# Sliding-window attention into a leaky-ReLU MLP: two zero fills moved from GpSimd to VectorE, one value cast shared between ScalarE and GpSimd, and one attention step placed a quarter tile later

## The chip, the core and the metric

The kernel runs on one core of a Trainium2 chip. The core has five engines that run their own instruction streams in order and wait for each other by semaphores: TensorE (PE; its weight loads are listed as PEld), VectorE (DVE), ScalarE (ACT), GpSimd (POOL) and SyncE (SP), which here only starts DMAs. The metric is device time in microseconds (us); the time before is the median of three runs.

## What is computed

Attention over a band of 32 positions on either side, for 8 batches, 8 heads, 576 positions and 64 values per head; then two dense layers with a leaky ReLU between, over all 4608 tokens:

```python
scores = scale * np.matmul(q, k.transpose(0, 1, 3, 2))
mask = np.abs(pos[:, None] - pos[None, :]) <= window      # window = 32
scores = np.where(mask, scores, -1000000000.0)
...
attn = attn / (np.sum(attn, axis=-1, keepdims=True) + 1e-09)
attn_out = np.matmul(attn, v)
x = attn_out.transpose(0, 2, 1, 3).reshape(B * S, H * D)   # 4608 x 512
h = x @ w_in                                              # 512 x 2048
g = np.maximum(0.01 * h, h)
out = g @ w_out                                           # 2048 x 512
```

## The kernel before

**Tiling.** Heads are taken in pairs (p = 0 to 3), and a batch's 576 positions in two halves of 288 tokens. An attention *step* i handles one pair in one half of one batch: batch i // 8, half (i // 4) % 2, pair i % 4; there are 64 steps. Keys and values of a pair lie block-diagonally: `kbd[b % 2]` and `vbd[b % 2]` are [128 partitions, pair, 9 blocks, 128], where head 0 fills the upper left 64 x 64 of each block, head 1 the lower right, and the rest must be zero. There are two copies of each, for even and odd batches. The copies for batch 0 are zeroed at the start (lines 134 to 137 and 158), those for batch 1 by POOL memsets of [128, 1152] in bf16: the four of `kbd[1]` and pairs 0 and 1 of `vbd[1]` at line 543, pairs 2 and 3 of `vbd[1]` at line 567. Later batches write only the diagonal parts again.

**A step** (`step`, line 420) issues: `join(i+1)` on DVE, which adds the two halves of the next step's masked scores (only from i = 11 on); `score(i+2)`, five matmuls into the single PSUM tile `ps`, the exponential on ACT (line 280) and the mask product on POOL (line 282); `sums(i)` on PE and the reciprocal on DVE (line 309); `product(i)`, five matmuls of `vbd` with the masked exponentials (line 320) into the single PSUM tile `x`; `scaled(i)` on DVE (line 334), which writes the attention output `xT`. Then keys that have arrived are copied into `kbd` on DVE (`place_keys`, line 258 for batches 0 and 1, line 260 later), and casts, transposes and loads of later batches are issued as `qk_due` and `v_due` tell (for batch 2 from step 9 on).

**Inputs.** Float32 loads are started by SP: `qf` and `kf` per pair, `vf` per pair in two transfers, one for each head. `cast_qk` casts queries on the engine given, else POOL, and keys on POOL (line 197); `cast_v` casts values into `vbd`, one instruction for each head, on ACT (line 203) or POOL (line 205). For batches 0 and 1 the cast tiles are transposed on PE (line 225) and copied out of PSUM by ACT (lines 233 and 239); from batch 2 on, DMAs transpose.

**The dense layers.** A group g is half a batch: 288 tokens, and 16 `h` tiles (line 348, four matmuls each) whose leaky ReLU ACT writes to `gT` (line 355). An `o` tile is 128 tokens by 512 outputs, 16 matmuls (line 390), copied out by ACT (line 395) and stored by SP. The `h` tiles, the `o` tiles, the transposes of PE and nothing else share four PSUM buffers (`mmps`). PE's order is that of the program text.

**The order around the change.** After group 0's tiles with steps 4 to 7 between them, DVE casts the queries of batch 1's pairs 0 and 1 (lines 558 and 559), and group 1's tiles follow (lines 560 to 569), with `second_pair(0)` and `second_pair(1)` behind tiles 7 and 11: transposes of a pair on PE, its copies on ACT, its keys' placing on DVE, then `cast_qk` of the pair two further on, queries on DVE and keys on POOL. The memsets of line 567 are issued behind tiles 7 and 9, and `score(8)` behind tile 13. From there a planned order runs: `plan` lists quarters of `o` tiles (four matmuls each) and `h` tiles; ahead of each `spend` is called. It counts the calls in `turn` and keeps a clock in estimated time; whenever the first entry of `due` has come, it issues the next step. `O_US` is the estimate for a quarter `o` tile. Step 8's entry is `4 * O_US`, which is the fifth turn, the first quarter of output tile 1; steps 9, 10 and 11 are at turns 8, 11 and 13. Ahead of steps 8 to 10 the values of pairs 1 to 3 of batch 1 are cast on ACT. The turns 1, 2 and 4 add `second_pair(2)`, `score(9)`, and `second_pair(3)` with the value cast of pair 0.

Of the kernel before, what the change touches and what calls it, by code (L numbers as in the profile page):

```python
# [16 lines left out]
def kernel(  # L17
# [14 lines left out]
    nc = tc.nc  # L32
# [54 lines left out]
    def load_v(b, p):  # L87

        t = fload.tile([128, NB, D], FP32, name=f"vf{p}")
        for a in range(2):  # L90
            nc.sync.dma_start(
                out=t[64 * a:64 * a + 64],
                in_=v[b, 2 * p + a].rearrange("(c p) d -> p c d", p=64),
            )
        vf[b, p] = t
# [25 lines left out]
    vbd = [const.tile([128, NPAIR, NB, 128], BF16, name=f"vbd{i}") for i in range(2)]  # L121
# [64 lines left out]
    def cast_qk(b, p, q_eng=None):  # L186
        for eng, src, dst in ((q_eng or nc.gpsimd, qf, qb), (nc.gpsimd, kf, kb)):
            if b < BY_DMA:
                parts = [(dst[:, p], src[b, p].rearrange("p a (c d) -> p c a d", d=D))]
            else:  # L190
                by_c = src[b, p].rearrange("p a (g c d) -> c p g a d", g=3, c=2)
                parts = [(dst[:, p, 3 * c:3 * c + 3], by_c[c]) for c in range(2)]
            for to, tok in parts:
                if eng is nc.scalar:
                    eng.activation(out=to, in_=tok, func=AF.Copy)
                else:
                    eng.tensor_copy(out=to, in_=tok)  # L197

    def cast_v(b, p, on_act=False, heads=range(2)):
        for a in heads:  # L200
            r = slice(64 * a, 64 * a + 64)
            if on_act:
                nc.scalar.activation(out=vbd[b % 2][r, p, :, r], in_=vf[b, p][r], func=AF.Copy)  # L203
            else:
                nc.gpsimd.tensor_copy(out=vbd[b % 2][r, p, :, r], in_=vf[b, p][r])  # L205
# [64 lines left out]
    def score(i):  # L270
        b, hf, p = where(i)
        by_c = qT[b][:, p].rearrange("p (c i) -> p c i", c=2)
        for n_, blocks in enumerate(WIN[hf]):
            for blk, i0, n in blocks:
                nc.tensor.matmul(  # L275
                    ps_v[:, n_, :, i0:i0 + n], kbd[b % 2][:, p, blk],
                    by_c[:, :, hf * EVEN + i0:hf * EVEN + i0 + n], start=True, stop=True,
                )
        e = attn.tile([128, 2 * HALF], BF16, name="e")
        nc.scalar.activation(out=e, in_=ps[:, P0:P0 + 2 * HALF], func=AF.Exp, scale=scale)  # L280
        pr = prob[:, i % NPROB]
        nc.gpsimd.tensor_mul(  # L282
            pr.rearrange("p n c i -> p (n c i)"), e, mask[hf].rearrange("p n c i -> p (n c i)"),
        )
        probs[i] = [pr, None, None]
# [60 lines left out]
    def h_mms(g, f, h, cs):  # L346
        for c in cs:
            nc.tensor.matmul(  # L348
                h[:, 0:HALF], w_in_bf[:, c, ts(f, 128)], xT[:, c, ds(g * HALF % RING, HALF)],
                start=(c == 0), stop=(c == DMC - 1),  # L350
            )

    def h_out(g, f, h):

        nc.scalar.activation(  # L355
            out=gT[:, f, ds(g * HALF % RING, HALF)].rearrange("p (i c) -> p i c", c=2),
            in_=h[:, 0:HALF].rearrange("p (c i) -> p i c", c=2), func=AF.Prelu, alpha=0.01,
        )

    def h_tile(g, f, n=1):  # L360

        hs = [mmps.tile([128, 512], FP32, name="mm", tag="mm") for _ in range(n)]
        for cs in (range(DMC - 1), (DMC - 1,)) if n > 1 else (range(DMC),):
            for i, h in enumerate(hs):
                h_mms(g, f + i, h, cs)
        for i, h in enumerate(hs):
            h_out(g, f + i, h)

    def h_first(g):

        hs = [mmps.tile([128, 512], FP32, name="mm", tag="mm") for _ in range(4)]
        yield hs[0]
        for c in range(DMC):
            for f in range(4):
                h_mms(g, f, hs[f], (c,))
            if c == DMC - 1:
                for f in range(4):
                    h_out(g, f, hs[f])
            yield
# [40 lines left out]
    def step():  # L420


        i = state["done"]
        if JOINED - 1 <= i < NC - 1:
            join(i + 1)
        if i < NC - 2:
            score(i + 2)
        weighted(i)
        place_keys()
        for b, p in qk_due.get(i, ()):  # L430
            cast_qk(b, p)
            transpose_dma(b, p)
            if 2 < b < B - 1:
                load_qk(b + 1, p)
        if 12 < i <= 12 + NPAIR:
            load_qk(3, i - 13)
        for b, p in v_due.get(i, ()):
            cast_v(b, p)
            if b + 1 < B:
                load_v(b + 1, p)  # L440
        state["done"] += 1
# [104 lines left out]
    def second_pair(p):  # L546
        next(second)
        next(second)
        place_keys()
        if p + 2 < NPAIR:  # L550
            cast_qk(1, p + 2, nc.vector)
            load_qk(2, p)
        if p == 1:
            load_qk(2, 2)
            load_qk(2, 3)

    second_half()
    cast_qk(1, 0, nc.vector)
    cast_qk(1, 1, nc.vector)
    for _ in h_first(1):  # L560
        pass
    for f in range(4, FFC):
        h_tile(1, f)
        if f in (7, 11):
            second_pair((f - 7) // 4)
        if f in (7, 9):
            nc.gpsimd.memset(vbd[1][:, (f - 3) // 2], 0.0)
        if f == 13:
            score(8)

# [3 lines left out]
    H_US, O_US, LEAD = 4 * (HALF / 2400 + 2.5e-3), 4 * 0.216, 4.0  # L574
# [9 lines left out]
    for us, kind, g, f in plan:  # L584
        if kind == "h" and f == 0:
            at[g] = t
        t += us
    due = [O_US * n for n in (4, 7, 10, 12)]
    for i in range(12, NC):
        prev = at[i // 4 - 1] - LEAD + (1.8 if i < 16 else 0)  # L590
        due.append(prev + (at[i // 4] - LEAD - prev) * (i % 4 + 1) / 4)
# [3 lines left out]
    def spend(us):  # L595
        nonlocal clock, turn
        while due and due[0] <= clock + 1e-6:
            due.pop(0)
            i = state["done"]
            if i < 11:  # L600
                cast_v(1, i - 7, on_act=True)
            step()
            if 10 <= i < 14:
                load_v(2, i - 10)
        turn += 1
        if turn == 1:
            second_pair(2)
        if turn == 2:
            score(9)
        if turn == 4:  # L610
            second_pair(3)
            cast_v(1, 0, on_act=True)
        clock += us

    for us, kind, g, f in plan:
        if kind == "h":
            spend(us)
            if f != 0:
                h_tile(g, f - 1, 2) if f == 1 else h_tile(g, f)
        elif f == 0:  # L620
            o_tile(g, lambda: spend(O_US))
# [28 lines left out]
```

## Time and profile before

| what | before |
|---|---|
| time, median of 3 runs | 320.3 us (319.94 to 320.85) |
| profiled execution, first to last instruction | 319.0 us |
| PE busy | 301.1 us (94%), granted clock 1.000 |
| DVE, ACT, POOL busy | 220.7, 183.5, 191.2 us |
| 0 to 36 us: PE busy | 24.30 us |
| 36 to 66 us: PE busy | 27.83 us |
| 300 to 319 us: PE busy | 15.82 us |

The profiled execution is not one of the three timed runs; its span is what its own instructions cover, and no separate time is recorded for it. All times within a run are counted from the span's start. A row of the order of time gives the start, the time from that start to the end of the last of its instructions, the engine, the source line, the operation, the tiles it writes and reads, and how many instructions are merged; in brackets stands how long the engine stood idle before and what ended that. Ends of matmuls are modelled, so neighbouring matmuls overlap in such rows, and a few matmul records are missing from the trace.

### The profile page before, as it was taken

Reading aid. Unit: us, or ns where it says so; the run is one execution under the profiler, and the core shown is the slowest. Engines: PE = TensorE matmul, PEld = TensorE weight load, DVE = VectorE, ACT = ScalarE, POOL = GpSimd, SP = SyncE. Lnnn points to the kernel's source line nnn. Section 1 sums busy time; section 2 is a strip of 40 time slices with the busy share of each in tenths; the row PEclk is TensorE's granted clock in tenths of the full one; section 3 lists DMA queues with packets and bytes.
Section 4 is the critical chain, followed back from the end, with each engine's and each line's share of the span. In section 5 each row is a group of like instructions: output and inputs, shape, how many; then the busy total and the mean of one; then the engine's idle time right before and its main releaser. Section 6 shows DMA issues by size and latency. Waiting matters only on the chain.

```text
span 319.0 us, 6455 instructions
## 1 busy us (share of the span) xinstructions
PE 301.1 (94%) x2429; PEld 203.5 (64%) x2449; DVE 220.7 (69%) x258; ACT 183.5 (58%) x394; POOL 191.2 (60%) x251
## 2 busy tenths in 40 slices
PE   2678998999999999999999999999999999999996
PEld 1457764576765858576765858576665858576653
DVE  5688886869755987688755987688745988565100
ACT  7686688574652828375552828465552837464531
POOL 7899963974646866585646866586637866330000
PEclk9999999999999999999999999999999999999999
DMA  8999998997998989399835996399833440000102
GB/s 189 224 184 229 269 242 188 242 200 180 223 245 167 245 148 210 79 237 202 173 76 114 233 229 151 74 215 223 178 76 104 108 71 33 35 35 2 66 31 71
DMA packets 108400, 49.46 MB, mean 155 GB/s; under 512 B 68816, under 2 KB 103888, under 8 KB 108368
## 3 DMA queue, kind: packets, MB, share of 16 engines
q1 hardware_dynamic: 104144, 44.84, 66.0%
q0 software_dynamic: 4224, 4.19, 8.1%
q8 instruction: 19, 0.31, 0.5%
q14 instruction: 13, 0.11, 0.1%
HBM read 36.70 MB, written 9.44 MB: 145 GB/s over the span
## 4 chain that ended last, share of the span: by engine, by line
PE 88%; DVE 5%; ACT 3%; issue 2%; POOL 1%; ACTq 0%; POOLq 0%; DVEq 0%
PE mm L390 38%; PE mm L348 37%; PE x L320 5%; PE ps L275 5%; PE s L301 2%; DVE r L309 2%; DVE qb L197 1%; PE s L304 1%; DVE kbd L258 1%; POOL prob L282 1%; ACT kT L239 1%; PE tp L225 1%; ACT e L280 1%; ACT vbd L203 1%; DVE kbd L134 1%
## 5 line engine op out<-in xcount | busy, mean ns | idle before, releaser
L309 DVE RECIPROCAL r<-s 128x288 f32<-128x288 f32 x64 | 125.2, 1956 | 57.0 <-PE s L301 53.3
L282 POOL TENSOR_TENSOR prob<-e,mask 128x576 bf16<-128x576 bf16 x64 | 81.6, 1276 | 89.2 <-ACT e L280 42.1
L348 PE MATMUL mm<-xT,w_in_bf 128*128 128x288 bf16 x1024 | 134.0, 286 | 0.1
L390 PE MATMUL mm<-w_out_bf,gT 128*128 128x512 bf16 (+2 forms) x572 | 128.7, 373 | 1.1
L355 ACT ACTIVATE gT<-mm 128x288 bf16<-128x288 f32 x256 | 101.2, 412 | 25.6 <-PE mm L348 9.1
L348 PEld LDWEIGHTS <-w_in_bf 128*128 128x128 bf16 x1024 | 98.4, 98 | 24.5 <-issue 0.3
L390 PEld LDWEIGHTS <-gT 128*128 128x128 bf16 x592 | 56.3, 98 | 59.2
L395 ACT ACTIVATE o_sb<-mm 128x512 f32<-128x512 f32 (+2 forms) x37 | 21.7, 585 | 91.8 <-PE mm L390 89.0
L280 ACT ACTIVATE e<-ps 128x576 bf16<-128x576 f32 x64 | 41.5, 648 | 10.6 <-PE ps L275 10.5
L197 POOL CAST kb<-kf 96x384 bf16<-96x384 f32 (+1 forms) x56 | 34.8, 643 | 4.5 <-DMA kf<-in_k_dram 4.3
L205 POOL CAST vbd<-vf 64x576 bf16<-64x576 f32 x50 | 34.7, 694 | 1.5
L334 DVE TENSOR_TENSOR xT<-x,r 128x288 bf16<-128x288 f32 x64 | 29.2, 457 | 7.8 <-PE x L320 1.1
L260 DVE COPY kbd<-kT 64x576 bf16<-64x576 bf16 x48 | 32.3, 674 | 0.6 <-DMA kT<-kb 0.3
L320 PE MATMUL x<-prob,vbd 128*128 128x128 bf16 (+2 forms) x320 | 26.0, 213 | 2.7 <-ACT vbd L203 1.3
L275 PEld LDWEIGHTS <-kbd 128*128 128x128 bf16 x320 | 20.8, 99 | 10.7 <-DVE kbd L258 1.6
L275 PE MATMUL ps<-qT,kbd 128*128 128x128 bf16 (+2 forms) x320 | 26.3, 214 | 1.3 <-DVE kbd L258 0.8
L197 POOL CAST qb<-qf 96x384 bf16<-96x384 f32 x48 | 24.4, 536 | 0.0
L320 PEld LDWEIGHTS <-vbd 128*128 128x128 bf16 x320 | 20.5, 99 | 5.4 <-ACT vbd L203 1.9
L292 DVE TENSOR_TENSOR both<-prob 128x288 bf16<-128x288 bf16 x52 | 20.0, 384 | 0.9
L301 PE MATMUL s<-both,ones_bd 128*128 128x288 bf16 x52 | 14.9, 286 | 0.0
L258 DVE COPY kbd<-kT 64x576 bf16<-64x576 bf16 x16 | 7.1, 446 | 6.2 <-ACT kT L239 6.0
L225 PE MATMUL tp<-ident,qb 96*128 96x96 bf16 x48 | 4.1, 233 | 6.8 <-DVE qb L197 6.8
(43 smaller groups left out, 87.9 us busy)
## 6 DMA issues: line engine op xcount, KB each, us to landing
qf<-in_q_dram SPq DMA_DIRECT2D x32, 288.0 KB, 4.6
kf<-in_k_dram SPq DMA_DIRECT2D x32, 288.0 KB, 5.3
vf<-in_v_dram SPq DMA_DIRECT2D x64, 144.0 KB, 4.4
out_dram<-o_sb SPq DMA_DIRECT2D x35, 256.0 KB, 3.9
w_in_bf<-in_moe_w_in_dram POOLq DMA_DIRECT2D x4, 512.0 KB, 8.2
w_out_bf<-in_moe_w_out_dram POOLq DMA_DIRECT2D x4, 512.0 KB, 16.4
qT<-qb SPq DMA_TRANSPOSE x24, 4.2
kT<-kb SPq DMA_TRANSPOSE x24, 3.1
```

Source lines behind the costliest of these rows:

```text
L197: eng.tensor_copy(out=to, in_=tok)
L205: nc.gpsimd.tensor_copy(out=vbd[b % 2][r, p, :, r], in_=vf[b, p][r])
L260: nc.vector.tensor_copy(out=to.rearrange("p n (m c) -> p n c m", c=2), in_=kT[r].rearrange("p (c n m) -> p n c m", c=2, n=NB),)
L275: nc.tensor.matmul(ps_v[:, n_, :, i0:i0 + n], kbd[b % 2][:, p, blk], by_c[:, :, hf * EVEN + i0:hf * EVEN + i0 + n], start=True, stop=True,)
L280: nc.scalar.activation(out=e, in_=ps[:, P0:P0 + 2 * HALF], func=AF.Exp, scale=scale)
L282: nc.gpsimd.tensor_mul(pr.rearrange("p n c i -> p (n c i)"), e, mask[hf].rearrange("p n c i -> p (n c i)"),)
L309: nc.vector.reciprocal(r, s)
L320: nc.tensor.matmul(x_v[:, :, i0:i0 + n], vbd[b % 2][:, p, blk, :], pr[:, n_, :, i0:i0 + n], start=(blk == parts[0][1]), stop=(blk == parts ...
L334: nc.vector.tensor_mul(place(i), x, r)
L348: nc.tensor.matmul(h[:, 0:HALF], w_in_bf[:, c, ts(f, 128)], xT[:, c, ds(g * HALF % RING, HALF)], start=(c == 0), stop=(c == DMC - 1),)
L355: nc.scalar.activation(out=gT[:, f, ds(g * HALF % RING, HALF)].rearrange("p (i c) -> p i c", c=2), in_=h[:, 0:HALF].rearrange("p (c i) -> ...
L390: nc.tensor.matmul(o[:, lo:hi], gT[:, f, ds(128 * j % RING, 128)], w_out_bf[:, f, lo:hi], start=(f == 0), stop=(f == FFC - 1),)
```

## The change

Three places change. The two memsets of pairs 2 and 3 of `vbd[1]` leave POOL's stream, where they stood among group 1's tiles, and are issued on DVE right behind its casts of the queries of pairs 0 and 1. The first entry of `due` becomes `5 * O_US`, so that step 8, with the value cast of pair 1 that goes ahead of it, is issued one turn later. And of the value cast of pair 0 in batch 1, head 0 stays on ACT while head 1 goes to POOL.

```diff
     cast_qk(1, 0, nc.vector)
     cast_qk(1, 1, nc.vector)
+    for p in (2, 3):
+        nc.vector.memset(vbd[1][:, p], 0.0)
     for _ in h_first(1):
         pass
     for f in range(4, FFC):
         h_tile(1, f)
         if f in (7, 11):
             second_pair((f - 7) // 4)
-        if f in (7, 9):
-            nc.gpsimd.memset(vbd[1][:, (f - 3) // 2], 0.0)
         if f == 13:
             score(8)
...
-    due = [O_US * n for n in (4, 7, 10, 12)]
+    due = [O_US * n for n in (5, 7, 10, 12)]
...
             second_pair(3)
-            cast_v(1, 0, on_act=True)
+            cast_v(1, 0, on_act=True, heads=(0,))
+            cast_v(1, 0, heads=(1,))
```

## The prediction

> **What bounds the kernel now.** I read the page's busy shares first (PE 94%, every other engine at 69% or less), then PE's busy time stage by stage, then who PE waited for, then each engine's order of time around those waits. By stage:
>
> ```profile
> 66.00:100.00 34.00, 33.84 (x273) 22.80 (x274) 25.04 (x30) 19.29 (x44) 18.57 (x24) 1.00 1.08 198
> 100.00:200.00 100.00, 99.68 (x803) 68.06 (x808) 77.36 (x93) 56.38 (x128) 68.19 (x91) 1.00 0.82 175
> ```
>
> The columns are stretch, length, then busy us of PE, its weight loads, DVE, ACT and POOL, granted clock, DMA share and GB/s. From 66 us on PE is busy without a hole, at clock 1.00, and no wait of PE is listed after 60 us. So work that PE starts earlier at 66 us ends earlier by as much. The change touches 35 to 52 us, and between 40 and 60 us PE waited twice:
>
> ```profile
> PE x L320 <- ACT vbd L203: 1.1, 1, 1.1
> PE tp L225 <- DVE qb L197: 0.7, 1, 0.7
> ```
>
> These are the first values product of batch 1 (step 8) waiting for its values, and the transposes of pair 2 waiting for DVE's cast of their queries. Those two waits are all that can be won. In order of time on PE:
>
> ```profile
> 45.07 0.43 PE L225 MATMUL tp<-ident,qb 96*128 96x96 bf16 x6 [0.66 <-DVE qb L197]
> 51.54 0.41 PE L320 MATMUL x<-prob,vbd 128*128 128x96 bf16 x5 [1.09 <-ACT vbd L203]
> ```
>
> **The fills.** DVE, and below it POOL, in that stretch:
>
> ```profile
> 37.74 1.17 DVE L197 CAST qb<-qf 96x768 bf16<-96x768 f32 x1
> 40.86 0.91 DVE L258 COPY kbd<-kT 64x576 bf16<-64x576 bf16 x2 [1.96 <-ACT kT L239]
> 41.80 3.21 DVE L197 CAST qb<-qf 96x768 bf16<-96x768 f32 x1
> 44.94 0.89 DVE L258 COPY kbd<-kT 64x576 bf16<-64x576 bf16 x2
> 45.86 2.11 DVE L197 CAST qb<-qf 96x768 bf16<-96x768 f32 x1
> ```
>
> ```profile
> 38.44 1.15 POOL L197 CAST kb<-kf 96x768 bf16<-96x768 f32 x1
> 41.79 0.82 POOL L197 CAST kb<-kf 96x768 bf16<-96x768 f32 x1 [2.19 <-DMA kf<-in_k_dram]
> 42.55 2.05 POOL L567 MEMSET vbd<- 128x1152 bf16 x2
> 45.50 0.82 POOL L197 CAST kb<-kf 96x768 bf16<-96x768 f32 x1 [0.90 <-DMA kf<-in_k_dram]
> ```
>
> The same DVE cast takes 0.64 us at its shortest (at 6.83 us) and 3.21 at 41.80. It ends at 45.01, 0.41 behind the end of POOL's fills (42.55 + 2.05 = 44.60). The cast at 37.74 ends at 38.91, 0.42 behind POOL's cast that ended at 38.49; the one at 45.86 ends at 47.97, 0.42 behind POOL's mask product that ended at 47.55. So DVE's cast stands still while POOL works, and comes out 0.42 us after it. With the fills gone from POOL, only the key cast (to 42.61) stands beside the cast at 41.80: it ends near 43.03 instead of 45.01. PE's work before the transposes ends at 44.41 (eight matmuls from 43.27, 1.14 us), so they start there and not at 45.07: **0.66 won**. What is late next: their PSUM buffers, which ACT empties with the last two of its copies until 45.00; the first of the two by about 44.6, when the second group of six transposes asks for it (44.41 + 0.26). I put that at 0, with 0.1 as its bound.
>
> On DVE the fills cost little. Its memsets of zero run as 32-bit words: 128x64 took 0.112 us, and the big one is
>
> ```profile
> 2.76 1.98 DVE L134 MEMSET kbd<- 128x2304 uint32 x1 [0.43 <-issue]
> ```
>
> which makes (1.978 - 0.112)/(2304 - 64) = 0.83 ns a word, so 576 words take 0.54 us, two 1.08: from 38.91 to 39.99. Were they as slow as POOL's (1.05 each), 41.01. What hides them is DVE's idle 1.96 us before 40.86, where it waits for ACT's first keys; at the slow bound the key copy comes 0.15 later, and the cast behind it has 1.38 to spare before 44.41. So 0 at both ends. Behind the fills on DVE stand only that copy and that cast. Nothing has read or written this part of vbd[1] before, so no wait is added. On POOL nothing else moves: the key cast at 45.50 and the mask products behind it hang on a DMA that lands at 45.47 (issued 28.67, 16.8 to landing).
>
> **The step, and the cast in halves.** ACT's order of time before:
>
> ```profile
> 49.43 0.65 ACT L239 ACTIVATE kT<-tp 128x576 bf16<-128x576 bf16 x1
> 50.09 1.39 ACT L203 ACTIVATE vbd<-vf 64x576 bf16<-64x576 f32 x2
> 51.51 0.60 ACT L395 ACTIVATE o_sb<-mm 128x512 f32<-128x512 f32 x1
> 52.13 1.39 ACT L203 ACTIVATE vbd<-vf 64x576 bf16<-64x576 f32 x2
> 53.54 0.65 ACT L280 ACTIVATE e<-ps 128x576 bf16<-128x576 f32 x1
> ```
>
> Step 8 before: score(10) on PE at 49.80, sums(8) at 50.04; product(8) could follow at 50.28 and came at 51.54, behind both casts: **1.26 lost**, more than the 1.09 listed because matmul ends are modelled. Moving the step from turn 5 to turn 6 puts four output matmuls (0.87 us, the step from 48.93 to 49.80) ahead of it. The step issues no DMA, and neither ACT's, DVE's, POOL's nor SP's order changes: it is moved past these four matmuls alone. New times, all 0.66 earlier to begin with: third pair's keys on ACT end at 49.42; the one half cast there ends near 50.12; the other half stands on POOL behind mask product 9 (47.68 + 1.42 = 49.10) and ends at 49.76 (0.66, the median of POOL's value casts; at their longest, 0.91, 50.01). Both halves of the source have landed by 48.7 (issued 31.27 and 33.52, 17.0 and 15.2 to landing). Step 8 now starts at 49.80 - 0.66 + 0.87 = 50.01, its product at 50.49: no wait. So the gross gain is 0.66 + 1.26 = **1.92**.
>
> **The new wait.** Between steps 8 and 9 there are now 8 matmuls (1.73) and not 12 (2.59), so score(11) comes at 50.73 + 1.73 = 52.46. It overwrites the scores that exp(10) reads, and exp(10) stands on ACT behind the half cast, one output copy and both casts for pair 1: 50.12 + 0.62 + 1.41 + 0.65 = 52.80. PE waits till about 52.85: **0.39 given back**. (Before, exp(10) ended at 54.19 and score(11) came at 54.38.) Product(9) also overwrites what scaled(8) reads. Reciprocal(8) starts with sums(8), at 50.70, ends at 52.66; scaled(8) ends at 53.23 if it follows as others do (0.10 after), in time for product(9) at 53.33. But before it came late:
>
> ```profile
> 53.58 0.46 DVE L334 TENSOR_TENSOR xT<-x,r 128x288 bf16<-128x288 f32 x1 [0.51 <-DVE r L309]
> ```
>
> 0.51 after its reciprocal, with nothing named as cause. If that comes again, product(9) waits 0.35 more. Steps 10 and 11 show 0.10, so I take none, and 0.35 as the bound. Behind step 9 there are 12 matmuls again; step 11 keeps the 0.32 it loses now (its product at 60.95, behind scaled(10), which ends at 60.90).
>
> **Sum:** -0.66 - 1.26 + 0.39 = -1.53 us; with the late scaling -1.18. Against the profiled span, 319.0 becomes 317.5. The runs shown have a median of 320.3 (319.94 to 320.85), 1.3 above that span; taking the same off it gives **318.8**.
>
> **Rivals.**
> *No new wait (0.14).* ACT reaches exp(10) in time, as when its copies come some tenths sooner: the whole 1.92 stays, 318.4. For it: the margin is 0.39 in a chain of five instructions. Against: ACT has no idle in it to give.
> *POOL's half is locked out (0.10).* DVE's key copies for pair 3 stand at about 49.5 to 50.4. If they get in ahead of POOL's cast as POOL gets in ahead of DVE's casts, the half ends at 50.4 + 0.66 = 51.1, product(8) waits 0.6, and exp(10) is then no longer last: 1.92 - 0.6 = 1.3 won, 319.0. For it: POOL's key cast takes 0.82 alone, 1.15 beside DVE's; against: the 16 copies of this kind never ran over 0.45, and POOL should start its cast 0.4 earlier than they. The Trainium skill, "SBUF — State Buffer", section "Who interferes with whom", says that DVE copies in a two-port mode and GpSimd instructions take a shared port pair for a whole instruction, and that whoever issues second is blocked fully; the 0.42 us above agree with it for DVE's casts, and no row here shows it for POOL's value cast behind a key copy.
> *The cast is not freed (0.12).* If the 3.21 is not the fills' doing, the transposes stay at 45.07, everything behind them is 0.66 later with its margins unchanged, and the gain is 1.26 - 0.39 = 0.87: 319.4. Against it stand the three 0.42s. Smaller versions, in which a later wait hides the rest, lie between that and 320.3 (0.06).
> *Slower (0.08): the transfers don't come earlier.* POOL's first query and key casts of batch 2 stand ahead of mask product 12, join(12) on DVE waits for that, and behind the join stand reciprocal(11) and scaled(11), which the last chunk of the next h tiles needs. The keys of that cast land at 56.7 (issued 51.48, 5.2 to landing); POOL would ask for them at 57.1 instead of 58.5. Scaled(11) would end at 62.3 and is needed at 63.85 (64.64 - 1.53 + 0.74), so a landing decides from 0.4 + 1.55 = 1.95 us later, and the kernel is slower from 1.95 + 1.53 = 3.5. With the 9.1 us that a load issued at 26.2 took, it lands 3.9 later: 320.7. For it: POOL waited 2.19 and 0.90 for such loads just before. Against: the loads' issue is not delayed by anything in the change.
>
> **How the numbers follow.** My forecast has 0.50. About 0.3% (0.96 us, down to 319.34) is what this measurement can tell from no change. The forecast and the first two rivals are faster: 0.74, less 0.02 for the edge of the third; the cast not freed and its smaller versions are the same: 0.18, plus 0.02; slower 0.08. Range 318.0 (all 1.92 and 0.36 for the spread of the runs before) to 320.2, which leaves out the slower case and the edges. The forecast's own range is 318.4 to 319.2.
>
> **What would show it.** Right: DVE's cast at 41.8 lasts about 1.2; the fills lie in 38.9 to 40.0; the transposes of pair 2 start near 44.4 unwaited; product(8) follows sums(8) by 0.24; score(11) waits for exp(10) some 0.4. Wrong: a cast still over 2 us, product(8) waiting for POOL, a wait on DVE's scaling at step 9, or any PE wait after 60 us that is not there now.

## The result and the profile after

The changed kernel takes 319.13 us (median of 5 runs, 318.88 to 319.14) against 320.3 (319.85 to 320.85): a ratio of 0.9963, 95% interval 0.995 to 0.9976, or 1.2 us less (0.8 to 1.6). The forecast was 318.8 in 318.0 to 320.2. The profiled span falls from 319.0 to 317.4.

The page's head and PE's busy time by stretch after (columns as before):

```profile
span 317.4 us, 6460 instructions
...
PE 301.6 (95%) x2429; PEld 204.0 (64%) x2449; DVE 218.3 (69%) x260; ACT 182.3 (57%) x393; POOL 189.3 (60%) x250
```

```profile
36.00:66.00 30.00, 29.56 (x255) 19.33 (x256) 20.83 (x26) 22.09 (x46) 19.35 (x26) 1.00 1.16 234
66.00:100.00 34.00, 33.84 (x262) 22.12 (x263) 25.62 (x32) 17.88 (x40) 19.91 (x26) 1.00 1.10 202
100.00:200.00 100.00, 99.68 (x813) 68.47 (x819) 76.74 (x92) 57.62 (x131) 66.42 (x90) 1.00 0.82 174
```

From 36 to 66 us PE is busy 29.56 us instead of 27.83; from 66 to 200 us its busy time is what it was (33.84 and 99.68). DVE in order of time, with the fills:

```profile
39.18 1.15 DVE L561 MEMSET vbd<- 128x576 uint32 x2
41.08 0.91 DVE L258 COPY kbd<-kT 64x576 bf16<-64x576 bf16 x2 [0.76 <-ACT kT L239]
...
42.02 1.18 DVE L197 CAST qb<-qf 96x768 bf16<-96x768 f32 x1
43.55 0.91 DVE L258 COPY kbd<-kT 64x576 bf16<-64x576 bf16 x2 [0.36 <-ACT kT L239]
44.49 0.56 DVE L197 CAST qb<-qf 96x768 bf16<-96x768 f32 x1
```

The two fills (line 561) take 1.15 us and end at 40.33, 0.75 before the key copy that waits for ACT. The cast of pair 2's queries, which took 3.21 us, takes 1.18, and that of pair 3's, which took 2.11, takes 0.56. PE around steps 8 and 9:

```profile
44.47 0.42 PE L225 MATMUL tp<-ident,qb 96*128 96x96 bf16 x6
...
50.05 0.40 PE L275 MATMUL ps<-qT,kbd 128*128 128x96 bf16 x5
50.29 0.41 PE L304 MATMUL s<-prob,ones_bd 128*128 128x288 bf16 x2
50.54 0.40 PE L320 MATMUL x<-prob,vbd 128*128 128x96 bf16 x5
50.77 1.89 PE L390 MATMUL mm<-w_out_bf,gT 128*128 128x512 bf16 x7
52.65 0.40 PE L275 MATMUL ps<-qT,kbd 128*128 128x96 bf16 x5
52.89 0.41 PE L304 MATMUL s<-prob,ones_bd 128*128 128x288 bf16 x2
53.31 0.40 PE L320 MATMUL x<-prob,vbd 128*128 128x96 bf16 x5
```

Neither wait of before is left. Product(8) follows sums(8) by 0.25. What is new is small: score(11) comes 1.88 behind the start of the eight matmuls that take 1.73, so it waits 0.15; product(9) comes 0.42 behind sums(9) and not 0.24, so it waits 0.18. ACT and DVE show for what:

```profile
49.49 0.68 ACT L203 ACTIVATE vbd<-vf 64x576 bf16<-64x576 f32 x1
50.08 0.57 ACT L395 ACTIVATE o_sb<-mm 128x512 f32<-128x512 f32 x1
50.55 1.37 ACT L203 ACTIVATE vbd<-vf 64x576 bf16<-64x576 f32 x2
51.95 0.65 ACT L280 ACTIVATE e<-ps 128x576 bf16<-128x576 f32 x1
```

```profile
50.74 1.96 DVE L309 RECIPROCAL r<-s 128x288 f32<-128x288 f32 x1 [0.27 <-PE s L304]
52.80 0.46 DVE L334 TENSOR_TENSOR xT<-x,r 128x288 bf16<-128x288 f32 x1
```

Exp(10) ends at 52.60 and score(11) starts at 52.65; scaled(8) ends at 53.26 and product(9) starts at 53.31.

One measure serves all runs below: the *stretch*, the time from the first transposes of batch 1 (line 225) to the first matmul of group 2's `h` tiles (line 348), both on PE. All that the change moves lies in it. It was 64.64 - 39.06 = 25.58 us and is 63.08 - 39.28 = 23.80: 1.78 less. Behind it the two profiled executions agree within 0.04 us (254.36 and 254.32); ahead of it the new one is 0.22 longer, which makes the span's 1.6. Each kernel has one traced execution, and that of before is one of its longer ones; what this does to the comparison stands under *The sum* below.

### The profile page after: what moved, and what is told of

It reads as the page before. It is cut to its first block, busy times and chain, and to the rows that moved or that the text cites. A ratio compares the mean times of both kernels' runs of the same rounds, so it can differ in the third digit from the quotient of the medians.

```text
span 317.4 us, 6460 instructions
## 1 busy us (share of the span) xinstructions
PE 301.6 (95%) x2429; PEld 204.0 (64%) x2449; DVE 218.3 (69%) x260; ACT 182.3 (57%) x393; POOL 189.3 (60%) x250
## 4 chain that ended last, share of the span: by engine, by line
PE 91%; DVE 4%; ACT 2%; issue 1%; POOL 1%; POOLq 0%; ACTq 0%; DVEq 0%
PE mm L348 39%; PE mm L390 38%; PE ps L275 5%; PE x L320 5%; PE s L301 2%; DVE r L309 2%; PE s L304 1%; PE tp L225 1%; ACT e L280 1%; POOL prob L282 1%; DVE kbd L134 1%; DVE kbd L258 1%; ACT kT L239 0%; ACT vbd L203 0%; DVE qb L197 0%
```

## The experiments

The ratio of each is to runs of the kernel before on the same chip. A stretch is read from the one traced execution, which need not be a typical one: for "all but the fills" it took 320.34 us (median 319.57), for the steps and batch 2's casts later 318.56 (median 320.6).

| kernel | stretch, us | median, us | ratio, 95% interval |
|---|---|---|---|
| before | 25.58 | 320.08 to 320.3 | 1 |
| changed | 23.80 | 319.13 | 0.9963 (0.995 to 0.9976) |
| changed, once more | 23.80 | 319.18 | 0.9966 (0.9953 to 0.9978) |
| fills only | 24.75 | 320.07 | 0.9991 (0.9979 to 1.0002) |
| all but the fills | 25.00 | 319.57 | 0.9985 (0.9975 to 0.9994) |
| cast whole on ACT | 24.60 | 319.92 | 0.9987 (0.9978 to 0.9997) |
| step 8 not later | 24.12 | 319.45 | 0.9977 (0.9967 to 0.9986) |
| fills in POOL's idle time | 24.21 | 319.52 | 0.9973 (0.9962 to 0.9984) |
| the same, two small DVE memsets | 23.80 | 319.13 | 0.9971 (0.9956 to 0.9986) |
| next value cast halved too | 23.80 | 319.14 | 0.9972 (0.9958 to 0.9986) |
| steps 9 to 11 later too | 23.16 | 319.04 | 0.9958 (0.9946 to 0.997) |
| ... and batch 2's casts later | 23.16 | 320.6 | 0.9997 (0.9967 to 1.0026) |
| batch 2's casts later alone | 24.55 | 319.84 | 0.9985 (0.9964 to 1.0005) |
| steps later, one pair's casts later | 23.16 | 320.78 | 1.002 (1.001 to 1.003) |

### The parts one by one

**Fills only.** Against the changed kernel:

```diff
-    due = [O_US * n for n in (5, 7, 10, 12)]
+    due = [O_US * n for n in (4, 7, 10, 12)]
...
-            cast_v(1, 0, on_act=True, heads=(0,))
-            cast_v(1, 0, heads=(1,))
+            cast_v(1, 0, on_act=True)
```

> Only the fills move to DVE; step 8 stays at turn 5 and both value casts of pair 0 stay on ACT. Measured by the stretch on PE from the first transposes of batch 1 to the first matmul of group 2: 25.58 us before (39.06 to 64.64), 23.80 in the changed kernel (39.28 to 63.08). Theory (the two waits are separate terms): the transposes of pair 2 start unwaited, 0.66 is won, product(8) still waits for ACT's two casts by 1.26: stretch 24.92, median near 319.6. Rival (once the keys come earlier the values come early enough too): stretch 23.8 to 24.0, median near 319.1. Rival (the 3.21 us cast is not the fills' doing): stretch 25.58, median 320.3.

Stretch 24.75, 0.83 won: the theory's 0.66 and 0.17 more. Product(8) still waits, 1.09 by the list. The transposes of pair 2 start at 44.47 as in the changed kernel, where that is 0.98 behind the start of the eight matmuls ahead of them (43.49), while the listed end of those is 1.14 behind; the idle time of 0.66 that was listed before was really 0.82. By the ratio the runs are only 0.29 us below before (0.06 above to 0.67 below), and by the medians 0.04 (320.07 and 320.11): in the median run moving the fills alone won nothing. More on that under *The sum*.

**All but the fills.**

```diff
-    for p in (2, 3):
-        nc.vector.memset(vbd[1][:, p], 0.0)
...
+        if f in (7, 9):
+            nc.gpsimd.memset(vbd[1][:, (f - 3) // 2], 0.0)
```

> The cast in halves and the later step, with the fills left on POOL where they were. Theory: the DVE cast of pair 2's queries again lasts about 3.2 us and the transposes behind it wait 0.66; product(8) waits for nothing, and step 9 keeps its two short waits (0.15 for exp(10), 0.18 for scaled(8)): stretch 23.80 + 0.66 = 24.46, median near 319.8. Rival (POOL's half of the cast is late, as the fills keep POOL busy): product(8) waits for POOL, stretch over 25.

Stretch 25.00 instead of 24.46. The cast lasts 3.19 again and the transposes wait for it. The rest comes from something that the expectation had left out, the pause before scaled(8) that the kernel before had shown; first DVE, then PE:

```profile
42.02 3.19 DVE L197 CAST qb<-qf 96x768 bf16<-96x768 f32 x1
...
54.01 0.46 DVE L334 TENSOR_TENSOR xT<-x,r 128x288 bf16<-128x288 f32 x1 [0.51 <-PE ps L275]
```

```profile
53.70 0.41 PE L304 MATMUL s<-prob,ones_bd 128*128 128x288 bf16 x2
54.52 0.40 PE L320 MATMUL x<-prob,vbd 128*128 128x96 bf16 x5 [0.41 <-DVE xT L334]
```

Product(9) waits for that scaling: 0.82 behind sums(9) instead of the changed kernel's 0.42, which is 0.40; its transposes of pair 2 start 0.79 later than the changed kernel's (45.27 - 39.29 against 44.47 - 39.28), the rest of the 1.20. POOL's half of the cast was in time (49.37 to 50.03), so the rival fell.

**The cast whole on ACT, and step 8 not later.** One edit each:

```diff
-            cast_v(1, 0, on_act=True, heads=(0,))
-            cast_v(1, 0, heads=(1,))
+            cast_v(1, 0, on_act=True)
```

> As the changed kernel, but both value casts of pair 0 on ACT. Theory: the second cast ends 0.68 later, near 50.85 in the changed kernel's time, so product(8) waits about 0.36; everything behind it on ACT is 0.68 later too, exp(10) ends near 53.28 and score(11) comes at 53.33, product(9) at 53.81 instead of 53.31: stretch 24.30, median near 319.6. Rival (the quarter tile alone covers the casts): stretch 23.80.

```diff
-    due = [O_US * n for n in (5, 7, 10, 12)]
+    due = [O_US * n for n in (4, 7, 10, 12)]
```

> As the changed kernel, but step 8 stays at turn 5. Theory: product(8) could come at 49.68 (in the changed kernel's time) and waits for ACT's half cast, which ends near 50.17: 0.5 lost; but with 12 matmuls to step 9 again neither exp(10) nor scaled(8) is late there, so 0.33 comes back: stretch 23.80 + 0.2 = 24.0, median near 319.3. Rival (the later step is worth its full quarter, 0.87): stretch 24.6.

With the cast whole, the stretch is 24.60, 0.3 above the theory: product(8) waits as expected (0.39 by its starts), but exp(10) ends at 53.63 and not at 53.28: from the start of pair 0's cast to the next cast behind it ACT needs 2.03 (49.54 to 51.57) and in the changed kernel 1.06 (49.49 to 50.55), 0.97 more and not 0.68. So half a cast is worth 0.80 us. With step 8 at its old turn the stretch is 24.12: product(8) waits 0.47 by the list, the waits at step 9 are gone, and 0.32 remains. The later quarter tile is worth 0.3, not its 0.87.

The run with step 8 not later also shows who holds up whom when DVE's cast comes first. DVE, then POOL:

```profile
42.02 0.56 DVE L197 CAST qb<-qf 96x768 bf16<-96x768 f32 x1
```

```profile
42.09 1.17 POOL L197 CAST kb<-kf 96x768 bf16<-96x768 f32 x1 [2.27 <-DMA kf<-in_k_dram]
```

Here the keys landed 0.07 us after DVE's cast had begun: DVE takes 0.56 and POOL's cast 1.17. In the changed kernel POOL's began at 41.96, 0.06 ahead of DVE's: POOL 0.82, DVE 1.18. The first to start runs at full speed, the other one waits for it. The Trainium skill says this in "SBUF — State Buffer", section "Who interferes with whom": the shared port pair goes to whoever issues first, for a whole instruction. The trace agrees, with these four numbers.

Which of the two is first is not fixed for a kernel. In the trace of the changed kernel once more (the last run below) DVE's cast began at 42.02 and took 0.56, and POOL's came second:

```profile
42.09 1.17 POOL L197 CAST kb<-kf 96x768 bf16<-96x768 f32 x1 [2.28 <-DMA kf<-in_k_dram]
```

### Why POOL, and what the pause is

**Fills in POOL's idle time.**

```diff
     for p in (2, 3):
-        nc.vector.memset(vbd[1][:, p], 0.0)
+        nc.gpsimd.memset(vbd[1][:, p], 0.0)
```

> As the changed kernel, but the two fills stay on POOL and are issued right behind its key casts of pairs 0 and 1, where POOL stands idle for 2.2 us until the next keys land. Theory A (what counts is that the fills no longer stand beside DVE's cast of pair 2): that cast lasts 0.6 to 1.2 us and the transposes behind it start unwaited, as in the changed kernel. Theory B (the pause of 0.5 us before DVE's scaling of step 8 comes with the place in DVE's instruction stream, which is again that of the kernel before): scaled(8) starts 0.5 after its reciprocal, product(9) waits 0.4 longer than in the changed kernel: stretch 24.2, median near 319.5. Rival to B (the pause came from the fills on POOL or from the late transposes): no pause, stretch 23.80, median near 319.1. Rival to A (the fills must leave POOL): stretch 24.6 or more.

**The same with two small instructions on DVE.**

```diff
     for p in (2, 3):
         nc.gpsimd.memset(vbd[1][:, p], 0.0)
+        nc.vector.memset(zero, 0.0)
```

> As the run before it (fills on POOL in its idle time), with two more instructions on DVE at the place where the changed kernel has its fills: memsets of one column that is zero already. They do nothing but move the instructions behind them two places on in DVE's stream. Theory B: the pause before scaled(8) is gone as in the changed kernel, stretch 23.80, median near 319.1. Rival: the stretch is that of the run before it, 24.2 if a pause was there.

The first gives 24.21, the second 23.80, as theories A and B had it. DVE's cast of pair 2 took 0.56 in both. Scaled(8) without and with the two small memsets:

```profile
53.09 0.46 DVE L334 TENSOR_TENSOR xT<-x,r 128x288 bf16<-128x288 f32 x1 [0.51 <-PE ps L275]
```

```profile
52.58 0.46 DVE L334 TENSOR_TENSOR xT<-x,r 128x288 bf16<-128x288 f32 x1
```

Without them it starts 0.51 behind its reciprocal (50.62 + 1.96 = 52.58), with them 0.10 (50.52 + 1.96 = 52.48). Their work is nothing; they move what follows two places on in DVE's stream. The other traces fit: scaled(8) starts 0.51 behind its reciprocal in the kernel before and in "all but the fills", which have no such two instructions, and 0.10 or 0.11 behind in all that have them. So the fills need not leave POOL, they need only not stand beside DVE's cast; and of the changed kernel's 1.78, 0.41 is the pause that two more instructions on DVE push elsewhere. In the changed kernel pauses of 0.48 and 0.47 stand before the scalings at 166.92 and 282.24, where PE waits for nothing. The Trainium skill, "Runtime: NRT & Kernel Launch", section "Instruction fetch mechanics", says that engines fetch instructions in blocks and that crossing a block's end is mostly hidden; a pause bound to a place in the stream fits that, but no run here counts instructions to a block's end.

### Step 9's new wait, and a better order

**The next value cast halved too.**

```diff
-                cast_v(1, i - 7, on_act=True)
+                cast_v(1, i - 7, on_act=True, heads=(0,) if i == 8 else range(2))
+                if i == 8:
+                    cast_v(1, 1, heads=(1,))
```

> As the changed kernel, but the next value cast too (pair 1, issued with step 8) is halved between ACT and POOL. Theory (two things are late at step 9, exp(10) and, behind it, scaled(8)): exp(10) ends 0.68 earlier and score(11) starts unwaited, but product(9) still waits for scaled(8), which doesn't move: stretch 23.80, nothing won. Rival (exp(10) alone is what step 9 waits for): stretch 23.5 to 23.65.

As the theory had it: score(11) starts unwaited at 52.50, product(9) at 53.31 as in the changed kernel, stretch 23.80. Two waits in a row, of which the later one alone decides.

**Steps 9 to 11 later too.**

```diff
-    due = [O_US * n for n in (5, 7, 10, 12)]
+    due = [O_US * n for n in (5, 8, 11, 14)]
```

> As the changed kernel, but steps 9, 10 and 11 come later too, at turns 9, 12 and 15 instead of 8, 11 and 13, so that 12 matmuls stand between any two of the steps 8 to 11. Theory (the short waits come from a distance of 8 matmuls): neither step 9 nor step 11 waits, which takes 0.33 and 0.32 off: stretch 23.15, median near 318.5. Rival (step 11 is now too late for the dense tiles of group 2, whose last chunk needs its output): a wait of PE on DVE's scaling of step 11 ahead of group 2's tiles, stretch 23.8 or more or a later wait of that size.

The stretch is 23.16: with 12 matmuls between steps none waits. But the median is 319.04, no better than the changed kernel's. DVE and PE behind it:

```profile
60.78 0.58 DVE L292 TENSOR_TENSOR both<-prob 128x288 bf16<-128x288 bf16 x1 [0.78 <-POOL prob L282]
```

```profile
63.84 0.90 PE L348 MATMUL mm<-xT,w_in_bf 128*128 128x288 bf16 x6 [0.38 <-DVE xT L334]
```

Join(12) waits 0.78 for mask product 12, which stands on POOL behind pair 0's casts for batch 2 (57.66 to 59.5), and reciprocal(11) and scaled(11) stand behind the join. This is the path of the rival that I had put on the slower side, with POOL's own queue in place of a late DMA. From the first transposes to score(14) it takes 25.17, the changed kernel 25.27.

**Batch 2's casts later, three ways.** All of them one step later, with the late steps and without; then those of pair 0 alone, with the late steps:

```diff
-        qk_due.setdefault(8 * (b - 1) + p + (1 if b == 2 else 2), []).append((b, p))
+        qk_due.setdefault(8 * (b - 1) + p + 2, []).append((b, p))
```

> The steps 9, 10 and 11 at turns 9, 12 and 15, and batch 2's query and key casts on POOL, with their transposes, one step later each (pair 0 behind step 10 instead of step 9, and so on). Measured to the first scores behind group 2's first tiles, score(14): 25.27 us from the first transposes of batch 1 in the changed kernel (39.28 to 64.55), 25.17 with the later steps alone, where join(12) waited 0.78 for POOL. Theory (what gave the later steps' gain back is mask product 12 standing on POOL behind pair 0's casts, with join(12), reciprocal(11) and scaled(11) behind it): join(12) doesn't wait, neither does PE before group 2's second pass, stretch to score(14) 24.62, median near 318.5. Rival (step 11 is too late by itself, reciprocal and scaling do not fit): PE still waits 0.3 or more on scaled(11), stretch 25.0 to 25.2. Rival (transposed keys of batch 2 now come too late): waits of DVE's key copies or of scores after 68 us.

> As the changed kernel, with only batch 2's query and key casts one step later each, the steps as they were. Theory: POOL's casts hide behind nothing that the changed kernel waits for, since join(12) didn't wait there: stretch to score(14) 25.27, median 319.1, nothing won. Rival (POOL's order alone costs time): 25.0 or less.

```diff
-        qk_due.setdefault(8 * (b - 1) + p + (1 if b == 2 else 2), []).append((b, p))
+        qk_due.setdefault(8 * (b - 1) + p + (1 if b == 2 and p > 0 else 2), []).append((b, p))
```

> Steps 9, 10 and 11 at turns 9, 12 and 15, and of batch 2's query and key casts only those of pair 0 one step later (behind step 10, where pair 1's stand already), so that mask product 12 stands ahead of them on POOL and the transposes of pairs 2 and 3 stay where they were. Theory: join(12) doesn't wait, PE has no wait behind step 8, stretch to score(14) 24.62 to 24.7 as with all casts later (39.28 to 63.98, 24.70), but without the late keys of pair 3 that DVE waited 1.1 for there; median near 318.5 and a narrow spread. Rival (the wide spread of times, 318.55 to 323.95, comes from the later steps or from the chip): spread as wide again.

All casts later with the late steps: to score(14) 24.70 (24.62 expected), and a profiled span of 316.9, the shortest here; but ten of its twelve runs go from 318.55 to 321.77, and two, at a granted clock of 0.995, took 322.92 and 323.95. In its profile PE waits for nothing from 60 us on, and DVE waits for transposed keys of batch 2:

```profile
80.16 1.03 DVE L260 COPY kbd<-kT 64x576 bf16<-64x576 bf16 x2 [1.09 <-DMA kT<-kb]
```

The casts later alone spread too (318.93 to 321.33), and in that profile PE's output matmuls waited 0.6 by the list for the load of `w_out`, which the edit doesn't touch. By the starts that is 0.74 (1.00 from the transposes ahead of them, 0.26 in the changed kernel), all but 0.01 of the 0.75 by which its stretch is longer. Less that wait score(14) would come at an estimated 25.28 (65.41 - 39.39 - 0.74), the theory's 25.27, unless the wait hides another. The late steps alone don't spread (318.81 to 319.28), nor does the last kernel (320.55 to 322.01, eleven of twelve up to 321.14). So long runs are most frequent with the later casts and transposes of pairs 1 to 3, but they come without them too: two of twelve with the two small memsets and two of ten with the next value cast halved took 1.0 to 2.1 us more than their median. Why was not seen.

With pair 0's casts alone moved, score(14) comes at 24.70 as well, and then more is lost than was won. Pair 0's and pair 1's casts now stand together on POOL ahead of mask product 13; DVE, then PE:

```profile
64.65 0.58 DVE L292 TENSOR_TENSOR both<-prob 128x288 bf16<-128x288 bf16 x1 [1.45 <-POOL prob L282]
```

```profile
72.11 0.28 PE L301 MATMUL s<-both,ones_bd 128*128 128x288 bf16 x1 [0.15 <-DVE r L309]
72.68 0.41 PE L320 MATMUL x<-prob,vbd 128*128 128x64 bf16 x5 [0.28 <-DVE xT L334]
...
76.99 0.28 PE L301 MATMUL s<-both,ones_bd 128*128 128x288 bf16 x1 [0.21 <-DVE r L309]
77.56 0.41 PE L320 MATMUL x<-prob,vbd 128*128 128x64 bf16 x5 [0.28 <-DVE xT L334]
...
82.61 0.40 PE L348 MATMUL mm<-xT,w_in_bf 128*128 128x288 bf16 x2 [0.45 <-DVE xT L334]
```

Join(13) waits 1.45, and from there DVE runs late through three steps, each of which now holds up PE: 1.37 in these five waits, and 2.27 in all behind score(14) (255.12 us to the end instead of 252.85). The theory had expected no such waits and a median of 318.5. No version tried is clearly faster than the changed kernel.

**The changed kernel once more**, beside the last:

> The changed kernel once more, on the same chip as the run before it. Theory: 319.1, about 1.0 to 1.2 below the kernel before, spread below 0.5.

The stretch is 23.80 to the hundredth; median 319.18, spread 0.74 where less than 0.5 was expected.

## Why the prediction was right, and where its sizes were off

*The fills.* Right in kind for the traced executions: DVE's cast came out 0.42 behind POOL's remaining key cast (41.96 + 0.82 = 42.78, then 43.20), and PE's transposes started unwaited. I took POOL's lead over DVE's cast for given, which it isn't, as the changed kernel's two traces show. The term of 0.66 was 0.82 in the trace, as the ends of PE's rows are modelled; I had seen this for the product (1.26 instead of 1.09) and not carried it over. The cost on DVE, 1.08 for both fills, was 1.15, and hidden.

*The step and the halves.* Product(8) waits for nothing, as forecast. The runs divide the gain: without halves 0.80 is lost, without the later turn 0.32.

*The new wait.* I took 0.39 for exp(10) and none for scaled(8), with 0.35 as bound. It was 0.15 and 0.18, in all 0.33. Exp(10) ended 8.13 behind the start of pair 2's transposes (52.60 - 44.47) and not 8.39 (52.80 - 44.41), as ACT's copies follow each other faster than I had counted. So product(9) came earlier than I had it, upon scaled(8), which was where I had put it (8.79 behind, forecast 8.82). A wait on DVE's scaling at step 9 stood among the signs of being wrong; it came, with 0.18, without the pause that I had in mind. The halved next cast shows that scaled(8), not exp(10), sets the end.

*The pause of 0.51.* I took none because two of three steps had none. That was right for the changed kernel by luck, as the reason, the place in DVE's stream, was one that I had not seen. With the fills on POOL it comes back.

*The sum.* -1.53 was forecast and -1.78 (stretch) or -1.6 (span) came in the trace, but the timed runs show only -1.2 and, the second time, -1.1 (0.7 to 1.5). The term that was off is the 1.3 us that I put between the profiled span and the runs. On record every timed run of the experiments has its own span, and each took 1.65 to 1.78 us longer than that span. So a span of 319.0 stands for a run of about 320.7, and the kernel before has such runs: of 99 beside the experiments, 64 took 319.84 to 320.20 us, 33 took 320.45 to 320.93, and two more (of the five beside the first result two, at 320.3, lie between). Its trace is one of the longer group, and I set it beside the median. With 1.7 in place of 1.3 my span of 317.5 gives 319.2; measured was 319.13.

What parts the two groups was not traced, but one cause fits the record. In the trace of before POOL's key cast began 0.01 us ahead of DVE's (41.79 and 41.80), and the fills stood right behind it. Where DVE's cast begins first, the fills come behind it and the wait of 0.82 should be gone. The changed kernel shows both orders, and the times agree: fills only has a median of 320.07, which is also that of the shorter group. Of the twelve runs of "all but the fills" nine took 319.31 to 319.85, with a median of 319.53, as with the fills in POOL's idle time (319.52); the other three took 320.15 to 320.34, and the traced one, with the wait, is one of them. And from the shorter group to the changed kernel it is 320.07 - 319.13 = 0.94, the stretch's 1.78 less 0.82 (0.96). So in about two of three runs moving the fills would win nothing by itself, and the rest of the change all of the 0.94. This is argued and not shown: no trace of a shorter run of before was kept, and two of ten runs with step 8 not later, where the fills are on DVE, were 0.5 above the median too.

## What to carry to other kernels

A fill costs nothing in an idle engine and up to 0.82 us here beside another engine's cast on the critical path: look at what runs on POOL whenever a DVE cast lasts longer than its shortest row, and move the POOL work in time before moving it to another engine. When steps are respaced, count for each step the chain that must end before the next (here sums, reciprocal and scaling ahead of the next product, 50.29 to 53.31, about 3 us) and the queue ahead of every link; each gap that was closed here opened the next one on POOL or DVE. Size a stall by the starts of the matmuls on either side, not by the listed idle time. And before a gain is read from one trace, compare its span with those of the timed runs: a trace of before that is not typical shows a wait that most runs may not have.

## What was not expected of the hardware

A pause of about 0.5 us on DVE belongs to a place in its instruction stream: two one-column memsets, 0.20 us of work, took 0.41 off the stretch by moving it. Which of two engines starts first, by 0.06 us, decides whether DVE's cast takes 0.56 or 1.18, and the order changes from one execution of a kernel to the next. And DVE's key copies of 64 x 576 in bf16 (line 258) were not held up by POOL's fill at all: with the fills in POOL's idle time (40.01 to 42.05) the two copies at 40.96 took 0.91, as they do with POOL idle.
